# One more key operand in DRAM, early operands for the second layer, and the last stores on another queue

## The chip, the cores and the metric

The kernel runs on one NeuronCore of a Trainium2 chip. The engines are TensorE (PE, matmuls; PEld is its weight loading), VectorE (DVE), ScalarE (ACT), GpSimd (POOL) and SyncE (SP). SP computes nothing and only issues transfers; POOL computes and also issues transfers. On-chip memory is SBUF, matmul results go to the eight banks of PSUM, and everything larger lies in DRAM. The metric is the time of one execution in microseconds (us), the median over several runs.

## What is computed

The input x has 2048 rows of 1024 columns, all arrays are 32-bit floats. Cut to what matters, the reference is:

```
xn = layernorm(x)
q, k, v = split heads of xn @ wqkv            # 32 heads of 32
pq, pk  = phi(q), phi(k)                      # phi(t) = (t+1 if t>0 else exp(t)) + 1e-6
kv  = pk^T v   per head;   z = sum of pk over rows
s   = (pq kv / (pq . z + 1e-6)) @ wo
h   = silu(xn @ w1) * (xn @ w3)               # 3584 columns
g   = silu(h @ w2)
out = x + s * g
```

## The kernel before

**Precision and products.** Every 32-bit operand is split into a high and a low part. `split` (L91) does this with one ACT instruction (L95, the high part) and one DVE instruction (L96, the low part). A product then takes three matmuls (L103 to L105). On top of that every large product is done in the seven block products of the Strassen-Winograd scheme, whose operands are blocks and sums of blocks (A11, S1 ... on one side, B11, T1 ... on the other; for the row products Y00, R2 ... in place of the B and T).

**Stages, in order of time.** The tokens are taken in two halves (h = 0, 1). For each half the keys, the queries and the hidden layer (gate w1, up w3) are computed by `gemm`. In the second half, after keys and queries, come the *row products* xn^T pk (`row_products`, L558): seven products in the order of `ROWS` (L625), each in four steps over the tokens. Then follow the hidden layer of the second half with the attention's small products beside it, the *attention* product s (the segment "s", 8 token groups m = 0 to 7), and the *second layer* h @ w2 in five segments of the hidden columns, B0 to B4, with the last segment also writing the output.

**The key operands.** `key_rows` (L519) turns each block of phi(k) by TensorE and stores operands of the row products in the DRAM tiles `y_d` through POOL (`keep_keys`, L516): Y00 at the first block, R5 and Y10 at another, Y01, R4 and R2 at the last (L549 to L554). Y00 is made at L536 in a buffer of the pool called `small` (tag "c", six buffers of 128x512). Those six also serve the intermediate results c22, c21 and c12 of `gemm`, r2, the results of the attention product, and raw operands of the second layer. The pool hands a buffer to its next user when its last user is done.

**The row products' loads.** A step of a row product loads two tiles of x operands and two of key operands with two transfers on SP's queue (`load`, L564) into one of two "raw" buffers, and splits them into eight smaller buffers (`ready`, L580). The last row product needs A11 and R2 − Y00. Y00 is loaded beside R2 into a "job" buffer (named yy; four such buffers, shared with the small jobs of the stage), and POOL subtracts it (L583) before the split. The loads named qd (L882, L884) and pqd (L847) belong to small jobs of the attention that run beside; wg is the first gate weight of the second half and uses a "raw" buffer too.

**Order.** The source is traced in order, and a planner then plays it through a simulated time line. On each engine it places the earliest traced instruction that is ready at that moment, and hands out buffers in this simulated order. So a load traced later can be issued earlier when its buffer is free. Each engine then executes its list strictly in order; SP's list holds most loads, POOL's most stores.

**From the attention to the second layer.** `Segment.right(k)` (L1016) splits seven right operands for the block k; `Segment.operands(m)` (L1023) loads and splits the seven left operands of the token group m. The first group of a segment runs "outer": for each k all seven products into seven banks. The right operands of the attention lie in the pool `pa`. The first seven of the second layer were traced after the attention (L1272), in the pool `pw`, which is laid over `pa`, `praw` and `st` after these are closed (L1260). `ask_first` (L1161) only requested four of the seven raw operands during the last attention group.

**The end.** `finish` (L1191) runs four times for each token group in the last segment, in the order (t, n) = (1,1), (0,0), (1,0), (0,1). It loads s and x (ss, xs), applies silu on ACT, multiplies and adds on DVE, and stores through POOL (L1202, or L1204, where the transfer itself adds).

Of the kernel before, what the change touches and what calls it, by code (L numbers as in the profile page):

```python
# [9 lines left out]
F32 = mybir.dt.float32  # L10
FR = mybir.dt.float32r
# [5 lines left out]
P = 128  # L17
C = 512
# [4 lines left out]
def tile_linear_attention_times_swiglu(  # L23
# [10 lines left out]
    nc = tc.nc  # L34
# [47 lines left out]
    s_d = [dram.tile([P, D], F32, name=f"s_d{t}") for t in range(S // P)]  # L82
    AOPS = ["A11", "S2", "S3", "S1", "A12", "A22", "S4"]
    XS = ["A11", "A12", "S1", "S3", "A22", "S2", "S4"]
    YS = ["Y00", "Y01", "Y10", "R5", "R2", "R4"]
    x_d = [dram.tile([P, TH // 2, len(XS), C], F32, name=f"x_d{h}") for h in range(NH)]
    y_d = [dram.tile([P, TH // 2, len(YS), ND // 2, P], F32, name=f"y_d{h}") for h in range(NH)]
    g_d = [dram.tile([P, ND // 2, C], F32, name=f"g_d{n}") for n in range(4)]
# [19 lines left out]
    pb = ctx.enter_context(tc.tile_pool(name="pb", bufs=8))  # L108
    pe = ctx.enter_context(tc.tile_pool(name="pe", bufs=3))
    pc = ctx.enter_context(tc.tile_pool(name="pc", bufs=6))  # L110
    era1 = ExitStack()
    pa = era1.enter_context(tc.tile_pool(name="pa", bufs=1))
    praw = era1.enter_context(tc.tile_pool(name="praw", bufs=2))
    st = era1.enter_context(tc.tile_pool(name="st", bufs=2))

    def small(name):
        return pc.tile([P, C], F32, tag="c", name=name)
# [4 lines left out]
    def job_tile(shape, name):  # L122
        return praw.tile(shape, F32, tag="job", bufs=4, name=name)
# [392 lines left out]
    def keep_keys(h, pair, n, t):  # L516
        nc.gpsimd.dma_start(out=y_d[h][:, :, YS.index(n), pair], in_=t.rearrange("p (t d) -> p t d", d=P))  # L517

    def key_rows(h, pair):  # L519

        rows = {}

        def use(n, c, src):
            j = 2 * pair + n
            pk = signed(f"pk{h}_{j}_{c}")
            z = st.tile([P, 1], F32, tag="z", name="z")
            phi(src, pk, z)
            nc.vector.scalar_tensor_tensor(zacc[:, j:j + 1], z, C * 1e-6, zacc[:, j:j + 1],
                                           op0=ALU.add, op1=ALU.add)
            later.append([3, lambda: turn(n, c, pk)])  # L530

        def turn(n, c, pk):
            V = nc.vector
            p_ = turned(pk, f"k{h}_{pair}_{n}{c}")
            if (c, n) == (0, 0):
                y00 = small(f"y00_{h}_{pair}")  # L536
                nc.scalar.activation(y00, p_, AF.Identity, bias=eps)  # L537
                keep_keys(h, pair, "Y00", y00)
            elif (c, n) == (1, 1):
                rows["y01"] = job_tile([P, 2, C], f"y01_{h}_{pair}")  # L540
                nc.scalar.copy(out=rows["y01"][:, 1], in_=p_)
            elif (c, n) == (1, 0):
                y10, r5 = (rows.setdefault("y10", job_tile([P, 2, C], f"y10_{h}_{pair}"))[:, e] for e in range(2))
                nc.scalar.activation(y10, p_, AF.Identity, bias=eps)
                V.tensor_sub(out=r5, in0=rows["y01"][:, 1], in1=p_)
                keep_keys(h, pair, "Y10", y10)
                keep_keys(h, pair, "R5", r5)
            else:
                (y01, r4), r5, r2 = (rows["y01"][:, e] for e in range(2)), rows["y10"][:, 1], small(f"r2_{h}_{pair}")  # L549
                nc.scalar.activation(y01, p_, AF.Identity, bias=eps)  # L550
                V.scalar_tensor_tensor(r4, p_, 2e-6, r4, op0=ALU.add, op1=ALU.add)
                V.scalar_tensor_tensor(r2, p_, 1e-6, r5, op0=ALU.add, op1=ALU.add)
                for n_, t in (("Y01", y01), ("R4", r4), ("R2", r2)):
                    keep_keys(h, pair, n_, t)  # L554

        return use

    def row_products():  # L558
# [3 lines left out]
        steps = [(i, *k) for i in range(len(ROWS)) for k in ks]  # L562

        def load(i, h, t):  # L564
            x_, y_, less = ROWS[i]
            raw = praw.tile([P, 4, C], F32, tag="raw", name=f"xy{i}_{h}{t}")

            def rows(dst, n):
                src = y_d[h][:, t:t + 2, YS.index(n)].rearrange("p t j d -> p t (j d)")
                nc.sync.dma_start(out=dst, in_=src)  # L570

            nc.sync.dma_start(out=raw[:, :2], in_=x_d[h][:, t:t + 2, XS.index(x_)])
            rows(raw[:, 2:], y_)
            other = None
            if less:
                other = job_tile([P, 2, C], f"yy{i}_{h}{t}")
                rows(other, less)
            return raw, other

        def ready(i, h, t):  # L580
            raw, other = data[i, h, t]
            if other is not None:
                nc.gpsimd.tensor_sub(out=raw[:, 2:], in0=raw[:, 2:], in1=other)  # L583
# [14 lines left out]
        for at, s in enumerate(steps):  # L598
# [408 lines left out]
    class Segment:  # L1007
# [5 lines left out]
            self.place, self.right_of, self.left_of, self.acc, self.end = place, right, left, acc, end  # L1013
            self.Y, self.X = {}, {}

        def right(self, k):  # L1016

            for i, n in enumerate(PRODUCTS):
                raw = self.right_of(n, i, k)
                self.Y[n, k] = self.place(n, i, k)  # L1020
                split(self.Y[n, k], raw)
# [141 lines left out]
            ask(i, n, k, small)  # L1163
        return asked[i, n, k]

    def ask_first():
# [21 lines left out]
    def added_by_dma(m, t):  # L1188
        return m < ADDED and t == 1

    def finish(m, t, n, a):  # L1191
        r0, cols = (2 * m + t) * P, slice(n * C, (n + 1) * C)
        ss = small(f"ss{m}_{t}{n}")
        nc.sync.dma_start(out=ss, in_=s_d[2 * m + t][:, cols])
        if not added_by_dma(m, t):
            xs = small(f"xs{m}_{t}{n}")
            nc.sync.dma_start(out=xs, in_=x[r0:r0 + P, cols])
        nc.scalar.activation(a, a, AF.Silu)
        nc.vector.tensor_mul(a, a, ss)
        if not added_by_dma(m, t):  # L1200
            nc.vector.tensor_add(a, a, xs)
            nc.gpsimd.dma_start(out=out[r0:r0 + P, cols], in_=a)  # L1202
        else:
            nc.gpsimd.dma_start(out=out[r0:r0 + P, cols], in_=a, accum_op=ALU.add)  # L1204

# [52 lines left out]
    assert all(next(j, None) is None for j, _ in jobs)  # L1258
# [17 lines left out]
    acc.extend(pw.tile([P, 2, 2, C], F32, tag=f"acc{m}", name=f"acc{m}") for m in range(NG))  # L1276
# [25 lines left out]
```

## Time and profile before

| what | value |
|---|---|
| median of 3 runs | 2360.43 us (2357.89 to 2363.99) |
| the profiled execution | 2364.7 us |
| its span, first to last instruction | 2362.9 us |
| mean granted TensorE clock | 0.992 |
| DRAM traffic | 308.81 MB read, 172.49 MB written |
| row products | about 917 to 1093 us of the span |
| attention product | about 1655 to 1809 us |
| second layer | 1809 to 2352 us |

The profile lists busy times by engine, then groups of instructions by source line, and who waited for whom. In a timeline a row has the start, the duration (of several merged instructions where "x4" stands), engine, line, operation, output and inputs, and in square brackets how long the engine was idle just before and what ended that. SPq is the queue in which SP issues transfers. Rows of stretches ("100.00:200.00") have the busy time of PE, PEld, DVE, ACT and POOL with their numbers of instructions, the granted clock of TensorE, the share of the DMA engines and GB/s.

### The profile page before, as it was taken

What the parts mean: (1) busy time and instruction counts of PE and PEld (TensorE: products, weight loads), DVE (VectorE), ACT (ScalarE), POOL (GpSimd) and SP (SyncE); (2) the same over time, 40 slices, a digit from 0 to 9 for tenths busy, and PEclk for the clock granted to TensorE, in tenths of its full rate; (3) what the DMA queues carried; (4) which work ended last, traced back from release to release, by engine and by line L of the source; (5) the groups of instructions that cost most, each with busy time, mean ns of one, the idle gap of its engine ahead of it and who ended that gap; (6) DMA issues with size and microseconds to landing.
All of it is one profiled execution on the core that took longest, in us unless ns stands there. A gap on an engine that the chain in (4) does not pass through costs nothing.

```text
span 2362.9 us, 30966 instructions
## 1 busy us (share of the span) xinstructions
PE 2306.2 (98%) x10368; PEld 1893.2 (80%) x10368; DVE 1775.7 (75%) x2822; ACT 924.5 (39%) x1639; POOL 697.2 (30%) x852
## 2 busy tenths in 40 slices
PE   6999999999999999998999999999999999999998
PEld 5788878888887888776888888888887788888876
DVE  8887888898877775656867688887745666767798
ACT  5555343423232555433233332334324534342433
POOL 5120433377866111012423435342310000000033
PEclk9999999999999999999999999999999999999999
DMA  6555455576669546776665567665756565766688
GB/s 236 165 174 178 156 179 183 172 228 220 225 210 321 196 134 205 255 257 207 201 193 181 188 200 218 195 216 168 230 153 195 181 198 172 225 208 182 191 265 260
DMA packets 354015, 479.69 MB, mean 203 GB/s; under 512 B 24144, under 2 KB 262736, under 8 KB 353744
## 3 DMA queue, kind: packets, MB, share of 16 engines
q1 hardware_dynamic: 316608, 359.20, 48.1%
q0 software_dynamic: 37248, 118.52, 15.2%
q8 instruction: 81, 1.33, 0.2%
q14 instruction: 78, 0.64, 0.1%
HBM read 308.81 MB, written 172.49 MB: 204 GB/s over the span
## 4 chain that ended last, share of the span: by engine, by line
PE 74%; DMA 5%; DVE 5%; issue 2%; ACT 1%; SPq 1%; POOL 0%; DVEq 0%; POOLq 0%; ACTq 0%
PE g L103 2%; PE g L104 2%; PE g L105 2%; PE cB L103 1%; PE cB L104 1%; PE cB L105 1%; PE dB L103 1%; PE dB L104 1%; PE dB L105 1%; PE aB L105 1%; PE aB L103 1%; PE aB L104 1%; DMA rA12B<-h_d 1%; PE bB L105 1%; PE bB L103 1%
## 5 line engine op out<-in xcount | busy, mean ns | idle before, releaser
L756 POOL DMA_DIRECT2D h_d<-sg x112 | 82.7, 739 | 262.5 <-DVE sg L752 183.9
L1069 POOL DMA_DIRECT2D u_d<-uB x32 | 17.3, 541 | 407.9 <-DVE uB L1052 354.8
L96 DVE TENSOR_TENSOR xy<-xy,xy 128x512 fp32r<-128x512 f32 x112 | 75.0, 704 | 70.4 <-ACT xy L95 70.2
L95 ACT CAST xy<-xy 128x512 fp32r<-128x512 f32 x112 | 65.1, 620 | 109.3 <-PE g L105 62.5
L103 PE MATMUL g<-xy,xy 128*128 128x512 f32 x224 | 82.3, 403 | 7.1 <-ACT xy L95 7.1
L104 PE MATMUL g<-xy,xy 128*128 128x512 f32 x224 | 88.5, 395 | 0.0
L105 PE MATMUL g<-xy,xy 128*128 128x512 f32 x224 | 87.9, 393 | 0.0
L517 POOL DMA_DIRECT2D y_d<-y x40 | 28.6, 718 | 141.9 <-ACT y L537 81.6
L1052 DVE TENSOR_TENSOR acc<-cB,acc 128x512 f32<-128x512 f32 x50 | 34.4, 688 | 40.2 <-PE cB L105 40.2
L1052 DVE TENSOR_TENSOR acc<-dB,acc 128x512 f32<-128x512 f32 x56 | 38.5, 688 | 31.0 <-PE dB L105 30.8
L736 POOL TENSOR_TENSOR hs<-hs,sg 128x256 f32<-128x256 f32 x56 | 61.1, 1090 | 0.1
L103 PEld LDWEIGHTS g<-xy,xy 128*128 128x128 f32 x224 | 42.1, 190 | 21.9 <-ACT xy L95 9.6
L738 POOL TENSOR_TENSOR hs<-sg 128x256 f32<-128x256 f32 x56 | 57.7, 1031 | 0.0
L894 POOL DMA_DIRECT2D qs_d<-qd x32 | 18.0, 564 | 119.3 <-DVE qd L890 82.0
L1183 POOL DMA_DIRECT2D s_d<-s x32 | 17.3, 541 | 117.7 <-DVE s L1052 70.9
L735 POOL TENSOR_TENSOR hs<-sg,sg 128x256 f32<-128x256 f32 x56 | 50.8, 906 | 1.2
L104 PEld LDWEIGHTS g<-xy,xy 128*128 128x128 f32 x224 | 42.7, 190 | 9.9 <-issue 0.8
L739 POOL TENSOR_TENSOR hs<-sg,hs 128x256 f32<-128x256 f32 x56 | 49.9, 892 | 1.5
L105 PEld LDWEIGHTS g<-xy,xy 128*128 128x128 f32 x224 | 42.6, 190 | 9.2
L771 POOL TENSOR_TENSOR w<-w 128x256 f32<-128x256 f32 x28 | 28.2, 1006 | 70.9 <-DMA w<-in_B_w 69.7
L764 POOL DMA_DIRECT2D h_d<-hs x60 | 45.8, 765 | 4.3 <-POOL hs L739 2.4
L674 POOL DMA_DIRECT2D pq_d<-pq x32 | 17.5, 546 | 91.1 <-DVE pq L507 88.3
(5315 smaller groups left out, 8330.1 us busy)
## 6 DMA issues: line engine op xcount, KB each, us to landing
h_d<-hs POOLq DMA_DIRECT2D x60, 256.0 KB, 3.5
h_d<-sg POOLq DMA_DIRECT2D x56, 256.0 KB, 3.9
w<-in_B_w SPq DMA_DIRECT2D x56, 256.0 KB
wt_d<-w SPq DMA_DIRECT2D x28, 512.0 KB
xy<-x_d SPq DMA_DIRECT2D x28, 512.0 KB
xy<-y_d SPq DMA_DIRECT2D x28, 512.0 KB
h_d<-hs SPq DMA_DIRECT2D x52, 256.0 KB
qs_d<-qd POOLq DMA_DIRECT2D x32, 384.0 KB, 3.9
```

The source lines that it names most:

```text
L95: nc.scalar.copy(out=hi, in_=src)
L96: return nc.vector.tensor_sub(out=lo, in0=src, in1=hi.bitcast(F32))
L103: nc.tensor.matmul(acc, lhsT=wh, rhs=ah, start=start, stop=False, skip_group_check=True)
L104: nc.tensor.matmul(acc, lhsT=wh, rhs=al, start=False, stop=False, skip_group_check=True)
L105: return nc.tensor.matmul(acc, lhsT=wl, rhs=ah, start=False, stop=stop, skip_group_check=True)
L735: e.tensor_add(out=s1, in0=a21, in1=a22)
L736: e.tensor_sub(out=s2, in0=s1, in1=a11)
L738: e.tensor_sub(out=s3, in0=a11, in1=a21)
L739: e.tensor_sub(out=s4, in0=a12, in1=s2)
L756: nc.gpsimd.dma_start(out=h_d[i][2 * h + c][:, 2 * n:4 * n + 2, k], in_=src)
L764: queue.dma_start(out=h_d[i][2 * h + c][:, 6 + 4 * e:10 + 4 * e, k], in_=o[e].rearrange("p (e s) -> p e s", s=P))
L1052: return V.tensor_add(out=c, in0=src, in1=c)
```

## The change

Four things are done together. (1) The key operand R6 = R2 − Y00 is computed on DVE in `key_rows`, in place in y00's buffer, and stored as a seventh operand in `y_d`; the row products no longer load Y00 beside R2 and POOL no longer subtracts. (2) `pa` is placed on the other side of SBUF and stays open during the attention, while `praw` and `st` are closed before it. In their place opens `pw0`, which has room for the second layer's seven right operands of k = 0 and the first accumulator. They are loaded and split during the attention groups 2 to 6, one or two in each. (3) In the last attention group four raw operands of k = 1 are requested, where it was k = 0. (4) In `finish`, the stores of (1,0) and (0,1) of the last token group go through SP's queue, and the two factors of the very last one are requested one call earlier.

```diff
-    YS = ["Y00", "Y01", "Y10", "R5", "R2", "R4"]
+    YS = ["Y00", "Y01", "Y10", "R5", "R2", "R4", "R6"]
...
-    era1 = ExitStack()
-    pa = era1.enter_context(tc.tile_pool(name="pa", bufs=1))
+    era1, era2 = ExitStack(), ExitStack()
+    pa = era2.enter_context(tc.tile_pool(name="pa", bufs=1, side="right"))
...
-                y00 = small(f"y00_{h}_{pair}")
+                y00 = rows["y00"] = small(f"y00_{h}_{pair}")
...
+                V.tensor_sub(out=rows["y00"], in0=r2, in1=rows["y00"])
+                keep_keys(h, pair, "R6", rows["y00"])
...
-            other = None
-            if less:
-                other = job_tile([P, 2, C], f"yy{i}_{h}{t}")
-                rows(other, less)
-            return raw, other
+            return raw
...
-            raw, other = data[i, h, t]
-            if other is not None:
-                nc.gpsimd.tensor_sub(out=raw[:, 2:], in0=raw[:, 2:], in1=other)
-            out = []
+            raw, out = data[i, h, t], []
...
-    ROWS = [("A22", "Y10", None), ("A12", "Y00", None), ("S2", "R2", None), ("S1", "R4", None),
-            ("S3", "R5", None), ("S4", "Y01", None), ("A11", "R2", "Y00")]
+    ROWS = [("A22", "Y10"), ("A12", "Y00"), ("S2", "R2"), ("S1", "R4"), ("S3", "R5"), ("S4", "Y01"), ("A11", "R6")]
...
-        def right(self, k):
-
-            for i, n in enumerate(PRODUCTS):
+        def right(self, k, some=range(7)):
+
+            for i in some:
+                n = PRODUCTS[i]
                 raw = self.right_of(n, i, k)
...
-            ask(0, n, 0, place)
+            ask(0, n, 1, place)
...
+    factors = {}
+
+    def fetch(m, t, n):
         r0, cols = (2 * m + t) * P, slice(n * C, (n + 1) * C)
-        ss = small(f"ss{m}_{t}{n}")
+        ss, xs = small(f"ss{m}_{t}{n}"), None
...
+        factors[m, t, n] = ss, xs
+
+    def finish(m, t, n, a):
+        r0, cols = (2 * m + t) * P, slice(n * C, (n + 1) * C)
+        if (m, t, n) not in factors:
+            fetch(m, t, n)
+        if (m, t, n) == (NG - 1, 1, 0):
+            fetch(m, 0, 1)
+        ss, xs = factors[m, t, n]
+        queue = nc.sync if m == NG - 1 and t != n else nc.gpsimd
...
-            nc.gpsimd.dma_start(out=out[r0:r0 + P, cols], in_=a)
+            queue.dma_start(out=out[r0:r0 + P, cols], in_=a)
...
-    run(attention, ahead=ask_first)
...
-    era1.close()
-    pw = ctx.enter_context(tc.tile_pool(name="pw", bufs=1, reuse_waits="tile"))
+    pw0 = ctx.enter_context(tc.tile_pool(name="pw0", bufs=1, reuse_waits="tile"))
+    pw = []
...
-        return pw.tile([P, 2, C], FR, tag=f"{n}_{k}", name=f"{n}_{k}")
+        return (pw[0] if k else pw0).tile([P, 2, C], FR, tag=f"{n}_{k}", name=f"{n}_{k}")
...
-    layers[0].right(0)
+
+    def first_weights(m):
+        if 2 <= m < NG - 1:
+            layers[0].right(0, [i for i in range(7) if i * 5 // 7 == m - 2])
+
+    run(attention, ahead=ask_next, around=first_weights)
     layers[0].operands(0)
+    era2.close()
+    pw.append(ctx.enter_context(tc.tile_pool(name="pw", bufs=1, side="right", reuse_waits="tile")))
...
```

More of the change, by code (lines that the diff above doesn't have):

```diff
@@ L564, in load @@
         def load(i, h, t):
-            x_, y_, less = ROWS[i]
+            x_, y_ = ROWS[i]
             raw = praw.tile([P, 4, C], F32, tag="raw", name=f"xy{i}_{h}{t}")
@@ L1164, in second_weights, with ask_next @@
         return asked[i, n, k]
-    def ask_first():
+    def ask_next():
         for n, place in zip(PRODUCTS, (spare, spare, small, small)):
-            ask(0, n, 0, place)
+            ask(0, n, 1, place)
     def spare(name):
@@ L1189, in added_by_dma @@
         return m < ADDED and t == 1
-    def finish(m, t, n, a):
+    factors = {}
+    def fetch(m, t, n):
         r0, cols = (2 * m + t) * P, slice(n * C, (n + 1) * C)
-        ss = small(f"ss{m}_{t}{n}")
+        ss, xs = small(f"ss{m}_{t}{n}"), None
         nc.sync.dma_start(out=ss, in_=s_d[2 * m + t][:, cols])
@@ L1256, in tile_linear_attention_times_swiglu @@
         attention.right(k)
-    run(attention, ahead=ask_first)
-    assert all(next(j, None) is None for j, _ in jobs)
+    era1.close()
     jobs.clear()
-    era1.close()
-    pw = ctx.enter_context(tc.tile_pool(name="pw", bufs=1, reuse_waits="tile"))
+    pw0 = ctx.enter_context(tc.tile_pool(name="pw0", bufs=1, reuse_waits="tile"))
+    pw = []
     def layer_place(n, i, k):
-        return pw.tile([P, 2, C], FR, tag=f"{n}_{k}", name=f"{n}_{k}")
+        return (pw[0] if k else pw0).tile([P, 2, C], FR, tag=f"{n}_{k}", name=f"{n}_{k}")
     acc = []
@@ L1271, in tile_linear_attention_times_swiglu @@
               for i, (f0, f1) in enumerate(FB)]
-    layers[0].right(0)
+    def first_weights(m):
+        if 2 <= m < NG - 1:
+            layers[0].right(0, [i for i in range(7) if i * 5 // 7 == m - 2])
+    run(attention, ahead=ask_next, around=first_weights)
     layers[0].operands(0)
+    era2.close()
+    pw.append(ctx.enter_context(tc.tile_pool(name="pw", bufs=1, side="right", reuse_waits="tile")))
     for k in range(1, layers[0].nk):
         layers[0].right(k)
-    acc.extend(pw.tile([P, 2, 2, C], F32, tag=f"acc{m}", name=f"acc{m}") for m in range(NG))
+    acc.append(pw0.tile([P, 2, 2, C], F32, tag="acc0", name="acc0"))
+    acc.extend(pw[0].tile([P, 2, 2, C], F32, tag=f"acc{m}", name=f"acc{m}") for m in range(1, NG))
     for i, seg in enumerate(layers):
```

## The prediction

> **What bounds the kernel now.** I read first the page's busy times, then who PE waits for, then the instruction timeline around each wait. The page says that PE is the bound:
>
> ```profile
> PE 2306.2 (98%) x10368; PEld 1893.2 (80%) x10368; DVE 1775.7 (75%) x2822; ACT 924.5 (39%) x1639; POOL 697.2 (30%) x852
> ```
>
> The change removes no matmul, so it can only win PE's idle time (2362.9 − 2306.2 = 56.7 us) and slow matmuls after it. The waits of PE (total, times, longest, in us) show which idle time the change touches:
>
> ```profile
> PE g L103 <- ACT xy L95: 7.1, 2, 6.9
> ...
> PE cB L103 <- ACT XS3B L95: 2.1, 2, 1.7
> ...
> PE T4B L103 <- ACT T L95: 1.2, 1, 1.2
> ...
> PE bg__9128 L103 <- ACT T2g__9056 L95: 1.0, 1, 1.0
> PE B11B L104 <- DVE B L96: 0.9, 1, 0.9
> PE B22B L103 <- ACT B L95: 0.8, 1, 0.8
> ```
>
> The first and fourth rows are the last row product, A11 times (R2 − Y00), and its exit. The other four are the start of the second layer. Of the 2.1 in the cB row only the longest, 1.7, lies there. Around the long wait PE's timeline reads:
>
> ```profile
> 1073.05 1.20 PE L103 MATMUL g<-xy,xy 128*128 128x512 f32 x4 [0.24 <-ACT xy L95]
> ...
> 1085.66 2.07 PE L103 MATMUL g<-xy,xy 128*128 128x512 f32 x4 [6.87 <-ACT xy L95]
> ...
> 1090.72 1.09 PE L103 MATMUL g<-xy,xy 128*128 128x512 f32 x4
> ...
> 1093.48 0.39 PE L103 MATMUL ag__9096<-A,B11g__9047 128*128 128x512 f32 x1
> ```
>
> The first row begins the third of four steps, the second the last. Twelve matmuls start between the second and third row (5.06 us), twelve between the third and fourth (2.76). So after the wait PE also runs slow and loses 5.06 − 2.76 = 2.3 us. This place costs 7.1 + 2.3 + 1.0 = 10.4 us.
>
> The Trainium skill, "TensorE: Matmul & The Clock Gate", section on the clock gate, says that the array drops to half clock after about 3.4 us without work and needs as long to come back. The 0.42 us per matmul after the 6.87 us wait against 0.23 later agrees. By that rule a wait merely shortened below 3.4 us already returns the 2.3 us.
>
> **Why the last step is late.** Timelines of POOL, DVE, SP's queue and ACT:
>
> ```profile
> 1055.64 2.39 POOL L583 TENSOR_TENSOR xy<-xy,yy 128x1024 f32<-128x1024 f32 x1 [16.46 <-DMA xy<-y_d]
> ...
> 1082.63 2.33 POOL L583 TENSOR_TENSOR xy<-xy,yy 128x1024 f32<-128x1024 f32 x1 [8.67 <-DMA xy<-y_d]
> ```
>
> ```profile
> 1058.71 3.35 DVE L96 TENSOR_TENSOR xy<-xy,xy 128x512 fp32r<-128x512 f32 x2 [4.13 <-ACT xy L95]
> ```
>
> ```profile
> 1037.29 0.36 SPq L570 DMA_DIRECT2D yy<-y_d  x1
> ...
> 1055.21 3.20 SPq L570 DMA_DIRECT2D yy<-y_d  x2
> ...
> 1063.29 0.36 SPq L572 DMA_DIRECT2D xy<-x_d  x1
> ...
> 1064.26 0.66 SPq L882 DMA_DIRECT2D qd<-r_d  x1
> ...
> 1071.29 1.08 SPq L572 DMA_DIRECT2D xy<-x_d  x1
> ...
> 1079.98 0.39 SPq L326 DMA_DIRECT2D wg__9019<-in_B_w  x1
> ```
>
> ```profile
> 1081.23 0.62 ACT L95 CAST xy<-xy 128x512 fp32r<-128x512 f32 x1 [7.20 <-DMA xy<-x_d]
> ...
> 1090.22 0.62 ACT L95 CAST B11g__9047<-wg__9019 128x512 fp32r<-128x512 f32 x1 [3.57 <-DMA wg__9019<-in_B_w]
> ```
>
> The last step's load goes out at 1071.29 because its buffer is freed late. Earlier steps wait for the POOL subtraction (2.4 us), and two DVE splits beside it take 3.35 us. It then goes out in the middle of the qd loads and its split starts ten microseconds later (1071.29 to 1081.23); then POOL subtracts again.
>
> **1. R6 stored as an operand.** Removed: four yy loads and four POOL subtractions. In each of the four steps the split starts without them.
>
> - The third step's load (1063.29) should move forward by the subtraction and its DVE delay, about 3 us, to 1060. The last one's buffer is then free when the second step is split, near 1064, and not at 1071. With the same ten microseconds of flight it lands by 1074.5; PE needs it 2.76 × 2 = 5.5 us after it starts the third step at 1073, at 1078.5. So the wait and the slow clock go.
> - yy's buffers come free for the qd loads from 1037 on. These take over yy's traffic there and leave the time of the last two loads.
> - What is late next: the first gate weights wg (1079.98), in the buffer of the third step. They come some nine microseconds earlier, as PE does, so T2g's wait of 1.0 need not vanish. I leave 0.3 of it. Gain: 10.4 − 0.3 = 10.1 us. Ends: 2.3 us (only the last subtraction goes from the last wait, and no load moves) and 10.4.
>
> Added: eight subtractions on DVE, eight stores on POOL, 2 MB written for the 2 MB no longer read. They follow L552; the windows are those around its first and last:
>
> ```profile
> L552 DVE SCALAR_TENSOR_TENSOR r<-trk,y x8: 679/681/682, 103.1 to 908.3; 128x512 f32<-128x512 f32 x8
> ```
>
> ```profile
> 100.00:200.00 100.00, 100.00 (x469) 82.75 (x468) 79.74 (x144) 56.17 (x95) 21.58 (x34) 1.00 0.53 171
> 800.00:900.00 100.00, 100.00 (x462) 82.58 (x461) 76.15 (x137) 55.79 (x95) 17.11 (x26) 1.00 0.41 132
> ```
>
> Eight times 0.68 is 5.4 us of DVE, hidden behind a PE that is 100% busy with DVE at 76 to 80%. Uncovered it would cost those 5.4. The eight stores are 8 × 0.82 = 6.6 us of POOL, at 17 to 22%; queued behind them are only further stores. I charge 0.3 us. y00 also keeps its buffer, one of six, from its own turn to R6's landing. The first and fourth Y00 store and the first R2 store in the first half:
>
> ```profile
> 77.80 0.73 POOL L517 DMA_DIRECT2D y_d<-y  x1 [18.08 <-ACT y L537]
> ...
> 89.83 0.71 POOL L517 DMA_DIRECT2D y_d<-y  x1 [1.86 <-ACT y L537]
> ...
> 104.14 0.82 POOL L517 DMA_DIRECT2D y_d<-r  x1
> ```
>
> A c22 lives from its first to its last use on DVE, about 6.4 us:
>
> ```profile
> 103.83 0.69 DVE L470 TENSOR_TENSOR c22k__1063<-ck__1020,uk__388 128x512 f32<-128x512 f32 x1
> ...
> 109.51 0.68 DVE L507 SCALAR_TENSOR_TENSOR pk<-c22k__1063,pk 128x512 f32<-128x512 f32 x1
> ```
>
> From 90 to 104 four y00 are live at once and two buffers are left for c22, c21, c12 and r2, of which one or two live at a time. It fits with nothing to spare: cost zero, the end a rival below.
>
> **2. First seven operands early.** Before, they wait for the attention's own buffers:
>
> ```profile
> 1806.11 0.62 ACT L95 CAST B<-rB11B 128x512 fp32r<-128x512 f32 x1
> ...
> 1813.17 0.62 ACT L95 CAST T<-rT4B 128x512 fp32r<-128x512 f32 x1 [2.22 <-DMA rT4B<-wt_d]
> ```
>
> ```profile
> 1809.08 0.68 DVE L96 TENSOR_TENSOR B<-rB11B,B 128x512 fp32r<-128x512 f32 x1
> ```
>
> ```profile
> 1829.31 0.38 SPq L1141 DMA_DIRECT2D rS3B<-h_d  x1
> ```
>
> ```profile
> 1700.00:1800.00 100.00, 100.00 (x443) 82.81 (x442) 44.80 (x69) 24.28 (x42) 10.81 (x20) 1.00 0.52 151
> ```
>
> Moved are seven loads (SP), seven ACT and seven DVE splits, 0.62 and 0.68 us each, into an attention where DVE is 45% and ACT 24% busy: 4.8 us of DVE, hidden; uncovered, that much. On SP they stand ahead of the left operands' loads. If one waits there for a small buffer, the next left operand waits too, and PE behind it; I charge 0.3. At the boundary the waits of 0.9, 1.2 and 0.8 = 2.9 us go. Late next is the second set of seven, which now arrives when the first did: first splits at 1809, the sixth (T4) at 1813.2 plus 0.7. PE, from 1809, needs its B11 after 21 matmuls of 0.23 = 4.8 us, at 1813.8, and its T4 15 matmuls later, at 1817. It holds by 3 us. The 1.7 us wait for S3's load is DVE and SP catching up; with 4.8 us less to do I take 1.0 of it. Gain 3.9; ends 0 (the second set takes the waits over) and 4.6.
>
> **3. The end.** The last two adds on DVE, the two stores on POOL, an SP issue and POOL's landing times:
>
> ```profile
> 2355.15 1.29 DVE L1201 TENSOR_TENSOR acc<-acc,xs 128x512 f32<-128x512 f32 x2
> ```
>
> ```profile
> 2356.13 1.14 POOL L1202 DMA_DIRECT2D out<-acc  x2 [2.65 <-DVE acc L1201]
> ```
>
> ```profile
> 2350.87 0.33 SPq L1197 DMA_DIRECT2D xs<-in_A_x  x1
> ```
>
> ```profile
> DMA to landing us min/median/max: 2.3/5.4/7.4
> ```
>
> ```profile
> 1814.26 4.58 DMA rT1B<-wt_d
> ```
>
> POOL ends its second issue at 2357.27; SP can start when the last add ends, 2356.44, and takes 0.33: 2356.77, a gain of 0.5. An SP store's landing is not shown. The nearest SP transfer, a load in traffic, took 4.58. Against POOL's shortest, 2.3, that turns the gain into a loss of 1.8; against its median, 5.4, it adds 0.8. I take 0.5, ends −1.8 and 1.3. The earlier fetch of two factors gains nothing: the multiply waits for ACT there.
>
> The Trainium skill, "DMA: Bandwidth & Descriptors", section "Issuing engines are not separate DMA queues", says that another issuing engine saves only its issue time. That is the 0.5; its table of first-byte latencies (about 1 us from GpSimd, 0.6 from SP) would make it an estimated 0.9. No run here shows an SP store's landing.
>
> **Sum:** 10.1 − 0.3 + 3.9 − 0.3 + 0.5 = 13.9 us. The profiled execution took 2364.7 (span 2362.9 and 1.8 around it), so 2350.8; it lies 4.3 above the median of the runs, 2360.4, whose prediction is 2346.5.
>
> **Rivals.**
> - *The row wait stays in part* (0.15). The qd loads, now earlier, meet the last two steps in SP's queue; for: SP's two yy issues took 3.2 us at 1055, so the queue was full. Against: they replace yy's bytes. With half the 6.9 us wait left and the clock as slow as now, 3.4 + 2.3 = 5.7 of the gain are lost: 2352.2; I put half of this case under 0.3%.
> - *The second set takes over the boundary's waits* (0.10), so that the pre-split does not do what it says: 3.9 less, 2350.4, still faster.
> - *Small buffers run short in the attention* (0.08): a raw operand waits for an s tile's store. At one product (12 matmuls, 2.8 us) in each of five groups it costs 14 us: 2360.5, no change. Against: two of six are free beside four s tiles.
> - *y00 fills the six buffers* (0.09), the slower one. If c22 must wait until R6 has landed, PE waits 0.68 + 0.82 + about 3 us (POOL stores land in 2.3 at least) = 4.5, plus 2.3 of slow clock = 6.8 per pair, eight pairs in the two halves 54 us: 2346.5 + 54 = 2401. It decides from two pairs on (14 us cancel the gain), and from four it is slower by over 0.3%. Against: the count above, and the queries between the keys of the second half.
>
> **Numbers.** The forecast has 0.58, 2341.5 to 2350: its best is 10.4 + 4.6 + 1.3 = 16.3, and runs scatter by 3 us either way (2357.9 to 2364.0). A change under 0.3%, 7.1 us, can hardly be told from none. Faster: 0.58 + 0.10 + half of 0.15 = 0.75; same 0.08 + 0.08 = 0.16; slower 0.09. The range runs from 2341.5 to 2357: it takes in the first two rivals with scatter and leaves out the last two, 0.17.
>
> **What would show it.** No yy load and no POOL subtraction; the last xy load issued before 1068 and no PE wait over 1 us in the last row product; no wait of B11B, T4B or B22B; DVE and ACT fuller between 1720 and 1790 with PE at 100%; SP issuing the last store. I am wrong if PE shows a new wait in the key stages, if the second set is late, or if other boundaries between layers, whose waits hang on the planner's order, move by several microseconds.

## The result, and the profile after

The changed kernel is slower. Its median is 2396.2 us (2394.0 to 2397.0) against 2362.2 us (2357.9 to 2368.6) for the kernel before in the same comparison: a ratio of 1.0135, with a 95% interval of 1.0113 to 1.0157. The profiled execution has a span of 2394.0 us, where it was 2362.9.

The waits that the change aimed at are gone all the same. First the page of the changed kernel (busy us, share of the span, instructions), then three of the rows that are left in its view of waits:

```profile
PE 2358.5 (99%) x10368; PEld 1897.7 (79%) x10368; DVE 1778.6 (74%) x2830; ACT 925.3 (39%) x1639; POOL 692.5 (29%) x854
```

```profile
PE bk__6499 L103 <- ACT T2k__6350 L95: 0.6, 1, 0.6
...
PE g L104 <- DVE xy L96: 0.5, 1, 0.5
...
PE cB L103 <- ACT XS3B L95: 0.2, 1, 0.2
```

The wait of 7.1 us in the last row product is down to 0.5. The rows for T2g, T4B, B11B and B22B are no longer there, and cB has 0.2 in place of 2.1. PE's idle time fell from 56.7 to 2394.0 − 2358.5 = 35.5 us, so 21 us were won. But PE's *busy* time rose from 2306.2 to 2358.5 us, by 52.3, for the same 10368 matmuls: 5.0 ns each on average. 52.3 − 21.2 = 31.1 us is the whole difference of the two spans.

Where do the slow matmuls lie? The view by stretches has the busy time and number of instructions of PE, PEld, DVE, ACT and POOL, then the granted clock, the share of the DMA engines and GB/s. Gate and up products of the first half's hidden layer (400 to 700 us, called the projections from here on) and second layer (1850 to 2250) of the kernel before:

```profile
400.00:700.00 300.00, 299.53 (x1330) 247.65 (x1328) 250.50 (x312) 101.91 (x172) 197.67 (x228) 1.00 0.63 206
1850.00:2250.00 400.00, 400.00 (x1766) 331.35 (x1765) 276.56 (x487) 154.04 (x299) 15.14 (x28) 1.00 0.63 193
```

The same view of the changed kernel, with the attention product between:

```profile
400.00:700.00 300.00, 300.00 (x1290) 241.83 (x1290) 243.91 (x305) 98.55 (x165) 189.85 (x218) 1.00 0.63 204
1700.00:1800.00 100.00, 99.70 (x426) 80.05 (x425) 54.63 (x85) 30.31 (x52) 13.00 (x24) 1.00 0.63 191
1850.00:2250.00 400.00, 399.31 (x1714) 321.85 (x1713) 263.61 (x471) 148.63 (x298) 16.75 (x31) 1.00 0.60 184
```

PE is as busy as before and its clock is full, yet it starts fewer matmuls: 1290 where it was 1330, 426 where it was 443, 1714 where it was 1766. The change adds no instruction between 400 and 700 us, so the cause is not local to the edits. It is also not everywhere. The timeline of the changed kernel, in the attention product and in the row products:

```profile
1749.68 0.39 PE L103 MATMUL as<-wp,XA12s 128*128 128x512 f32 x1
...
1755.76 0.40 PE L105 MATMUL ds<-wp,XS4s 128*128 128x512 f32 x1
```

```profile
1074.70 0.39 PE L104 MATMUL g<-xy,xy 128*128 128x512 f32 x1
...
1079.00 0.39 PE L105 MATMUL g<-xy,xy 128*128 128x512 f32 x1
```

In the attention 26 matmuls start between the two rows' starts, 6.08 / 26 = 0.234 us apart. In the row products it is 19 in 4.30 us, 0.226 apart. The duration shown, 0.39 to 0.40, is the same in both. The row products are the stage in which both operands lie in one pool.

### The profile page after: what moved, and what is told of

Same layout as the page of the kernel before. It is cut to its first block, busy times and chain, and to the rows that moved or that the text cites. A ratio compares the mean times of both kernels' runs of the same rounds, so it can differ in the third digit from the quotient of the medians.

```text
span 2394.0 us, 30980 instructions
## 1 busy us (share of the span) xinstructions
PE 2358.5 (99%) x10368; PEld 1897.7 (79%) x10368; DVE 1778.6 (74%) x2830; ACT 925.3 (39%) x1639; POOL 692.5 (29%) x854
## 4 chain that ended last, share of the span: by engine, by line
PE 91%; DVE 4%; DMA 3%; issue 1%; ACT 1%; SPq 1%; DVEq 0%; ACTq 0%
PE g L103 2%; PE g L104 2%; PE g L105 2%; PE dB L104 2%; PE dB L103 2%; PE cB L103 2%; PE dB L105 2%; PE aB L105 2%; PE cB L105 2%; PE cB L104 2%; PE aB L104 2%; PE aB L103 2%; PE bB L103 1%; PE bB L105 1%; PE bB L104 1%
## 5 line engine op out<-in xcount | busy, mean ns | idle before, releaser
L750 POOL DMA_DIRECT2D h_d<-sg x112 | 82.8, 740 | 270.0 <-DVE sg L746 175.8
L517 POOL DMA_DIRECT2D y_d<-y x48 | 34.6, 721 | 143.8 <-ACT y L537 82.1
L103 PEld LDWEIGHTS g<-xy,xy 128*128 128x128 f32 x224 | 41.8, 188 | 13.9 <-issue 3.7
L95 ACT CAST XS4B<-rS4B 128x384 fp32r<-128x384 f32 (+1 forms) x40 | 19.7, 492 | 61.7 <-PE cB L105 42.5
```

The source lines that it names most:

```text
L95: nc.scalar.copy(out=hi, in_=src)
L103: nc.tensor.matmul(acc, lhsT=wh, rhs=ah, start=start, stop=False, skip_group_check=True)
L750: nc.gpsimd.dma_start(out=h_d[i][2 * h + c][:, 2 * n:4 * n + 2, k], in_=src)
```

## The experiments

The addresses below are those at which the allocator places the pools, in bytes of a partition. A matmul has a *stationary* operand, loaded as weights; here these lie in the pool `pb` (L108), which begins at byte 17,984 in both kernels. The *moving* operand lies in `pa` or `pw`; in the change that of the second layer's block k = 0 lies in `pw0`, on the left. Before, `pa` begins at 77,376 on the left side. With `side="right"` it ends at the right end, byte 229,344, and as it holds 7 × 16,384 bytes it begins at 114,656. In the row products both operands lie in `pb`. No trace shows these addresses. The 59,392 bytes from `pb` to `pa` before can be added up from the pools in the source (8 × 4,096 + 3 × 2,048 + 10 × 2,048), and b_pad416 below counts on from there.

**First set: alignment, side, or order?** Theory A: 114,656 is no multiple of 64, 77,376 is one, and a moving operand off a multiple of 64 is read more slowly. Rival B: the right side itself is the cause. Rival C: the new order of the work is (more VectorE and ScalarE work beside the matmuls). An unused tile at the right end, of 32, 64 or 96 bytes, shifts the pool:

```diff
+    edge = ctx.enter_context(tc.tile_pool(name="edge", bufs=1, side="right"))
+    edge.tile([P, 8], F32, name="edge")        # 8, 16 or 24 floats
     pa = era2.enter_context(tc.tile_pool(name="pa", bufs=1, side="right"))
```

> The changed kernel with an unused 32-byte tile at the right end of SBUF, so that pa and later pw start at byte 114624 (a multiple of 64) and not at 114656 (32 past one). Theory A, matmuls are slower when the moving operand does not start on a multiple of 64 bytes: 8232 of the 9792 matmuls of 512 columns get back some 6.4 ns each, 53 us, so about 2343 us, with a spacing of 0.227 us between matmuls as in the kernel before. Rival B, the right side of SBUF itself is slow, by its place and not its alignment: no change, 2396 us, spacing 0.233. Rival C, the slowness comes from the new order of instructions: no change, 2396 us.

> The changed kernel with an unused tile of 64 bytes in the same place: pa moves by twice as much but stays 32 past a multiple of 64. Theory A: no change, 2394 to 2398 us, spacing 0.233. If a shift as such helped, because neighbouring addresses or the planner's order change: about 2343 us as with 32 bytes.

> The changed kernel with 96 bytes: pa starts on a multiple of 128, where the kernel before and the variant with 32 bytes start 64 past one. Theory A with 64 bytes as the unit: 2343 us as with 32 bytes. If 128 bytes were the unit and 64 past one only half good: faster than with 32 bytes, spacing below 0.226, each 0.005 us worth 41 us.

In the kernel before, 8 floats fewer in an unused tile among the constants shift all pools by 32 bytes, so that both operands leave the multiples of 64:

```diff
-    const.tile([P, 79], F32, name="gap")
+    const.tile([P, 71], F32, name="gap")
```

> The kernel before with its unused tile of 79 numbers made 71, so that every later tile moves down by 32 bytes and all operands, moving and stationary, start 32 past a multiple of 64. Nothing else changes. Theory A: all 9792 matmuls lose about 6.4 ns, 63 us: about 2425 us, with the row products slow too (spacing 0.233, in the changed kernel 0.227). Rivals B and C: no change, 2362 us.

Measured, against 2364.0 us for the kernel before: 2385.9 us with 32 bytes (ratio 1.0090, 1.0075 to 1.0105), 2391.8 with 64 (1.0114, 1.0099 to 1.0129), 2363.3 with 96 (0.9996, 0.9986 to 1.0006), and 2365.0 for the kernel before, shifted (1.0005, 0.9996 to 1.0015). The view by stretches of the kernels with 32 and with 96 bytes:

```profile
400.00:700.00 300.00, 300.00 (x1301) 243.37 (x1300) 247.15 (x309) 100.81 (x169) 192.63 (x223) 1.00 0.63 204
```

```profile
400.00:700.00 300.00, 299.51 (x1317) 245.60 (x1316) 249.41 (x310) 101.62 (x171) 199.96 (x228) 1.00 0.63 204
```

All three explanations fall. An aligned moving operand (32 bytes) is still slow, and a misaligned one (the kernel before, shifted) is not slow at all, so A is out. Side and order are the same in the three shifted kernels (PE and SP execute the same list), yet the time moves by 28 us among them, so neither B nor C can be the cause of that. What did stay the same in the shifted kernel before is the *distance* between the two operands. That gives theory D: the distance between moving and stationary operand sets the spacing of matmuls. Before, it is 77,376 − 17,984 = 59,392 = 232 × 256; in the change 114,656 − 17,984 = 96,672 = 377 × 256 + 160. All tiles in both pools are whole multiples of 512 bytes, so each pair of operands in them has the same remainder. From here on this remainder is called the distance: 0 before, 160 in the change. (The expectations still count it modulo 512.)

**Second set: the distance alone.** The first kernel keeps all of the change and brings the distance back to 0 with 416 bytes at the right end; a small tile moves into the constants to make room. The second has nothing of the change but its distance:

```diff
 # a_edge416, on the changed kernel
-    const.tile([P, 79], F32, name="gap")
+    const.tile([P, 63], F32, name="gap")
+    mom_c = const.tile([P, TH, 2], F32, name="mom")
...
+    edge.tile([P, 104], F32, name="edge")
     pa = era2.enter_context(tc.tile_pool(name="pa", bufs=1, side="right"))
...
-            mom = st.tile([P, TH, 2], F32, tag="mom", bufs=1, name="mom")
+            mom = mom_c
```

```diff
 # b_pad416, on the kernel before
-    const.tile([P, 79], F32, name="gap")
+    const.tile([P, 63], F32, name="gap")
...
+    shift = ctx.enter_context(tc.tile_pool(name="shift", bufs=1))
+    shift.tile([P, 104], F32, name="shift")
     pa = era1.enter_context(tc.tile_pool(name="pa", bufs=1))
```

> The changed kernel with an unused tile of 416 bytes at the right end of SBUF, so that the moving operands lie a whole number of 2048 bytes from the stationary ones, as in the kernel before (to make room, the 64-byte tile mom is taken from the gap of the constants). Theory D (what slows the matmuls is the distance between moving and stationary operand, modulo 512 bytes: 0 before, 416 in the change): matmul starts 0.226-0.227 us apart in every stage, as before; PE busy back at 2306-2310 us; and the waits stay gone, so the time is that of before less the 21 us by which PE's idle time shrank in the change: 2340-2348 us. Rival E (the distance is one cause, but the denser VectorE and ScalarE work beside the attention product is another): the attention stage stays at 0.229 us or more, and the time is 2352-2363 us.

> The kernel before with an unused tile of 416 bytes ahead of the moving operands' pool, on the left side where that pool was (64 bytes of it taken from the gap of the constants): nothing of the change in it but the distance of 416 bytes modulo 512. Theory D: matmul starts 0.232 us apart in the projections and 0.2335-0.2355 in attention and layers, PE busy up by some 45-55 us, time 2405-2418 us, slower than the change itself, since before's waits are still there. Rival E and every rival that blames the side, the order or the neighbours: 2358-2368 us, spacing 0.2267.

The changed kernel at distance 0 took 2343.0 us against 2363.3 for the kernel before: ratio 0.9917, 0.9902 to 0.9932. The kernel before at the change's distance took 2416.2 us: ratio 1.0227, 1.0212 to 1.0242. Busy times and stretches of the first:

```profile
PE 2299.1 (98%) x10368; PEld 1890.0 (81%) x10368; DVE 1779.0 (76%) x2830; ACT 923.3 (39%) x1639; POOL 687.5 (29%) x854
```

```profile
400.00:700.00 300.00, 300.00 (x1332) 248.17 (x1331) 251.72 (x311) 101.76 (x172) 194.50 (x228) 1.00 0.64 208
1850.00:2250.00 400.00, 400.00 (x1766) 331.04 (x1764) 284.00 (x490) 149.71 (x287) 22.91 (x34) 1.00 0.64 197
```

and of the second:

```profile
PE 2364.9 (98%) x10368; PEld 1896.7 (79%) x10368; DVE 1776.4 (74%) x2822; ACT 925.9 (38%) x1639; POOL 694.6 (29%) x852
```

```profile
400.00:700.00 300.00, 300.00 (x1291) 241.35 (x1290) 242.84 (x307) 98.40 (x166) 190.94 (x220) 1.00 0.61 203
1850.00:2250.00 400.00, 397.86 (x1696) 319.15 (x1696) 266.01 (x476) 156.49 (x312) 16.21 (x30) 1.00 0.61 191
```

The matmul counts of the projections follow the distance: 1332 with the whole change at distance 0, 1291 without any of the change at the change's distance (1330 and 1290 above). As the first has the side and the order of the change, B and C are out altogether. Rival E, VectorE's load beside the matmuls, asked for 2352 us or more at distance 0 and falls too. The effects add up: 2416.2 − 2363.3 = 52.9 us from the distance, 2363.3 − 2343.0 = 20.3 us back from the rest, together 32.6 slower, where 34.0 was measured.

Two further distances, with 352 and 224 bytes at the right end:

```diff
+    edge.tile([P, 88], F32, name="edge")       # a_edge352; 56 in a_edge224
```

> The changed kernel with 352 bytes at the right end: distance 64 modulo 512. Theory D does not say by itself how the cost runs with the distance. If any distance but 0 costs like those run so far (384, 352 and 416: spacing 0.230-0.235), 2380-2396 us. If the cost falls as the distance leaves the weights' end (320 gave 2363 us), it is cheap here: 2343-2365 us. Rival E as for a_edge416, 2352 us or more in any case.

> The changed kernel with 224 bytes at the right end: distance 192 modulo 512. As for the distance of 64: 2380-2396 us if every distance but 0 costs the same, 2343-2365 us if distances that are far from 352-416 are cheap, as 320 was.

They took 2364.1 us (1.0002, 0.9992 to 1.0011) and 2390.5 us (1.0112, 1.0095 to 1.0128). So not every distance but 0 costs the same: 64 costs about 21 us against distance 0, 192 about 47.

**Third set: whose distance, and with what period?** In the kernel before, only the pool of the stationary operands is moved, 192 bytes down; every other pool stays:

```diff
-    const.tile([P, 79], F32, name="gap")
+    const.tile([P, 31], F32, name="gap")
...
     pb = ctx.enter_context(tc.tile_pool(name="pb", bufs=8))
+    shift = ctx.enter_context(tc.tile_pool(name="shift", bufs=1))
+    shift.tile([P, 48], F32, name="shift")
```

> The kernel before with its stationary operands' pool moved 192 bytes down (the gap of the constants is cut by 192 bytes and an unused tile of 192 bytes follows the pool): the moving operands and every other pool keep their addresses, and all operands of the matmuls stay on multiples of 64 bytes. Theory D with the stationary operand as the partner: spacing 0.231 us in the projections and 0.233 us in attention and layers, as in the changed kernel at a distance of 192, and 2400-2412 us; the row products, whose two operands move together, stay at 0.226-0.227. If the partner is not the stationary operand but what VectorE, ScalarE or the DMAs touch in the other pools (rival F), the distance to those is as before: 2358-2368 us.

It took 2409.7 us, ratio 1.0197 (1.0182 to 1.0212). Its stretch in the projections:

```profile
400.00:700.00 300.00, 300.00 (x1295) 241.57 (x1294) 245.03 (x307) 98.88 (x166) 192.09 (x220) 1.00 0.63 204
```

1295 matmuls, as in the changed kernel at the same distance (1296). The moving operands had kept their addresses and their distance to the other pools, so rival F falls. One form of it is left, as VectorE and ScalarE also write into `pb`. A stretch of the same run in which neither they nor GpSimd work, and two of its matmuls:

```profile
466.85:470.15 3.30, 3.30 (x16) 2.67 (x15) 0.00 (x0) 0.00 (x0) 0.00 (x0) 1.00 0.37 108
```

```profile
466.72 0.40 PE L103 MATMUL cg__3940<-A,T4g__3840 128*128 128x512 f32 x1
...
470.22 0.39 PE L103 MATMUL dg__3941<-S,B22g__3868 128*128 128x512 f32 x1
```

Fifteen matmuls start in 3.50 us, 0.233 apart, as in the rest of that run. So the partner is the stationary operand. The row products, whose two operands moved together, kept the mean of the kernel before, 0.228. The period is tested with 160 bytes at the right end, where the distance modulo 512 is 256:

```diff
+    edge.tile([P, 40], F32, name="edge")       # a_edge160
```

> The changed kernel with 160 bytes at the right end: distance 256 modulo 512. Distances of 64 and 320 gave the same spacing in each stage (0.227 and 0.229 us), which speaks for a period of 256 bytes: then 256 is as good as 0, spacing 0.2267, and the time 2340-2348 us. If the period is 512 bytes, a distance of 256 puts the two streams half a weight row apart and costs like 192 or 352: 2380-2396 us.

It took 2344.1 us, ratio 0.9915 (0.9902 to 0.9928), and its row has the count of distance 0:

```profile
400.00:700.00 300.00, 299.97 (x1331) 248.05 (x1330) 248.53 (x310) 101.45 (x172) 195.79 (x228) 1.00 0.64 207
```

So among the distances tried the period is 256 bytes. All kernels of the three sets by the distance, with the matmuls between 400 and 700 us, and the mean from one matmul's start to the next in the attention, where every moving operand lies in `pa` (586 to 588 intervals; waits left out):

| distance | matmuls in 300 us | mean in the attention, us | kernels | time of the changed kernel at that distance |
|---|---|---|---|---|
| 0 | 1325 to 1332 | 0.227 | before, before shifted by 32, change with 416, with 160 | 2343.0, 2344.1 us |
| 64 | 1317, 1318 | 0.229 | change with 96, with 352 | 2363.3, 2364.1 |
| 96 | 1296 | 0.233 | change with 64 | 2391.8 |
| 128 | 1301 | 0.233 | change with 32 | 2385.9 |
| 160 | 1290, 1291 | 0.234 | change, before with 416 | 2396.2 |
| 192 | 1296, 1295 | 0.233 | change with 224, before with `pb` moved | 2390.5 |

**The same inside one kernel.** In the changed kernel `pw0` opens on the left, where `praw` began, at 77,376: its distance is 0. The second layer starts with 21 matmuls from `pw0`. Ahead of them stands the attention (`pa`), behind them block k = 1 (`pw`), both at 160:

```profile
1832.61 0.39 PE L103 MATMUL ds<-wp,XS4s 128*128 128x512 f32 x1
...
1835.19 0.40 PE L105 MATMUL ds<-wp,XS4s 128*128 128x512 f32 x1
...
1836.58 0.39 PE L105 MATMUL T2B<-T,XS2B 128*128 128x512 f32 x1
...
1839.97 0.39 PE L105 MATMUL B22B<-B,XS4B 128*128 128x512 f32 x1
1840.20 0.40 PE L103 MATMUL B11B<-B,XA11B 128*128 128x512 f32 x1
...
1841.84 0.40 PE L103 MATMUL T1B<-T,XS1B 128*128 128x512 f32 x1
```

Eleven intervals in the first 2.58 us are 0.235 each, fifteen between 1836.58 and 1839.97 are 0.226, and seven behind them 0.234. The first three from `pw0` are still 0.231 to 0.235, so a change of pool is felt for some matmuls. Later in the layer matmuls from `pw0` mostly come three at a time between those from `pw`, and there the mixture costs too. At distance 64 the layer of a_edge352 starts 1728 matmuls where a_edge416 starts 1766, 0.2315 us apart on average:

```profile
1850.00:2250.00 400.00, 400.00 (x1728) 324.50 (x1727) 272.47 (x479) 149.74 (x290) 14.59 (x27) 1.00 0.61 190
```

About 9 of the 21 us that distance 64 costs lie in this layer (548.0 us from its first to its last matmul, 539.4 in a_edge416).

**What the parts are worth at distance 0.** Two kernels undo one part each on a_edge416. The first splits the second layer's first operands after the attention again, the second forms R2 − Y00 on GpSimd again:

```diff
 # e416_no_early
-            ask(0, n, 1, place)
+            ask(0, n, 0, place)
...
-    run(attention, ahead=ask_next, around=first_weights)
+    run(attention, ahead=ask_next)
+    layers[0].right(0)
```

```diff
 # e416_no_r6
-                V.tensor_sub(out=rows["y00"], in0=r2, in1=rows["y00"])
-                keep_keys(h, pair, "R6", rows["y00"])
...
+            if less:
+                other = job_tile([P, 2, C], f"yy{i}_{h}{t}")
+                rows(other, less)
...
+            if other is not None:
+                nc.gpsimd.tensor_sub(out=raw[:, 2:], in0=raw[:, 2:], in1=other)
...
-    ... ("S4", "Y01"), ("A11", "R6")]
+    ... ("S4", "Y01", None), ("A11", "R2", "Y00")]
```

> The changed kernel at distance 0, with the second layer's first seven operands split after the attention product again (places kept). By the prediction's term the early splits are worth 3.9 us less 0.3: 2345-2349 us, with waits of 0.9 + 1.2 + 0.8 us before the first matmuls of the layer. If most of the 20 us that the change brings at distance 0 come from here, 2353 us or more.

> The changed kernel at distance 0, with the key operand R6 formed from R2 and Y00 on GpSimd again. By the prediction's terms R6 is worth 10.1 us less 0.3: 2350-2355 us, with the wait of some 7 us before the last step of the row products back, and half the clock behind it. If the wait alone counts and not the slow clock, 2349 us.

They took 2347.0 us (0.9927, 0.9916 to 0.9939) and 2356.7 us (0.9970, 0.9958 to 0.9981). Against the 2343.0 of a_edge416, from the second set, the early operands are worth 3.9 us and R6 13.7; by the ratios to the kernel before of each set, 0.0010 and 0.0053, it is 2.4 and 12.5. The intervals of the ratios leave some 4 us either way, so the part of the early operands is not told from nothing by the medians alone. The traces are sharper: from its first B11B matmul to its last matmul the second layer takes 543.5 us without the early operands (1790.82 to 2334.27) and 539.4 with them, 4.1 less. Of the other kernels at distance 0, two without early operands took 543.7 and 543.4 us (before, before shifted), two with them 536.8 and 538.0 (a_edge160, e416_no_r6). Waits came back at and shortly behind the start of the layer (1796 and 1824 us), though not the same ones as before (line numbers are one higher here). Without the early operands:

```profile
PE T4B L104 <- ACT T L96: 2.0, 1, 2.0
...
PE dB L104 <- ACT XS4B L96: 1.1, 1, 1.1
```

and without R6, where the first and third row are those of the prediction:

```profile
PE g L104 <- ACT xy L96: 7.2, 2, 6.6
...
PE cg__2661 L104 <- DVE c22g__2693 L473: 2.1, 1, 2.1
...
PE bg__9132 L104 <- ACT T2g__9060 L96: 1.1, 1, 1.1
```

For R6, 2356.7 us lies above the expected 2350 to 2355: the 12.5 to 13.7 us stand against some 7 to 12. Where the rest comes from is read off below.

## Why the prediction was wrong, and where it was right

The forecast was 2346.5 us and "faster"; measured was 2396.2, outside the range. **The step that failed** is the sentence under the first row: "The change removes no matmul, so it can only win PE's idle time". Apart from slow matmuls behind waits, it took the busy time of PE as fixed. The change moved `pa` to the other side, the distance to `pb` went from 0 to 160 modulo 256, and PE's busy time grew by 52.3 us. The side of `pa` was in the diff, but it had no term in the sum, no rival, and none of the signs of being wrong that the prediction names. The slower rival, that y00 fills the six buffers, named nearly this time (2401) with another mechanism, by chance: the stretches it spoke of are full, and only their matmul counts fell (469 and 462 before):

```profile
100.00:200.00 100.00, 100.00 (x458) 81.13 (x457) 79.95 (x145) 55.49 (x93) 24.38 (x38) 1.00 0.55 178
800.00:900.00 100.00, 100.00 (x452) 80.98 (x451) 78.56 (x139) 55.40 (x94) 21.11 (x32) 1.00 0.44 139
```

**The other steps** can be judged at distance 0, where only they are left. There the change gave 20.3 us by the medians and 22.2 by the spans, where 13.9 was predicted. The starts of five matmuls, first in the kernel before, then in a_edge416, show in which stage:

```profile
917.64 0.39 PE L103 MATMUL g<-xy,xy 128*128 128x512 f32 x1
...
1673.44 0.39 PE L103 MATMUL as<-wp,XA11s 128*128 128x512 f32 x1
...
1808.27 0.39 PE L103 MATMUL B11B<-B,XA11B 128*128 128x512 f32 x1
...
2351.99 0.39 PE L105 MATMUL dB<-B,XS4B 128*128 128x512 f32 x1
```

```profile
912.18 0.39 PE L104 MATMUL g<-xy,xy 128*128 128x512 f32 x1
...
1078.99 0.39 PE L104 MATMUL ag__9104<-A,B11g__9055 128*128 128x512 f32 x1
...
1657.25 0.39 PE L104 MATMUL as<-wp,XA11s 128*128 128x512 f32 x1
...
1791.21 0.39 PE L104 MATMUL B11B<-B,XA11B 128*128 128x512 f32 x1
...
2330.57 0.39 PE L106 MATMUL dB<-B,XS4B 128*128 128x512 f32 x1
```

(The row for ag in the kernel before, 1093.48, stands in the prediction.)

| stretch | before | a_edge416 | won | predicted |
|---|---|---|---|---|
| start to the row products | 917.6 | 912.2 | 5.5 | −0.3 |
| row products | 175.8 | 166.8 | 9.0 | 9.4, with the slow clock |
| hidden layer, second half | 580.0 | 578.3 | 1.7 | 0.7, of T2g's wait |
| attention | 134.8 | 134.0 | 0.9 | −0.3 to 0 |
| second layer | 543.7 | 539.4 | 4.4 | 3.9 |
| last matmul to the end | 10.9 | 10.1 | 0.8 | 0.5 |

- *R6.* Its place in the row products was right, wait and slow clock, within 0.4 us. So was the way to it. The stage's last x load goes out at 1061.24, where it was 1071.29. Of these 10.05 us the earlier start of the stage makes 5.5, so 4.6 are won (the prediction had 7), and the load's split starts at 1070.89, 9.65 us behind it (predicted ten).

  Too small was the term as a whole: 10.1 − 0.3 against 12.5 to 13.7. The missing part lies ahead of the row products, where the first row-product matmul starts at 912.2 with R6 and at 919.8 without it. Single traces scatter here: of the kernels at distance 0, three with R6 start it between 911.6 and 912.2, three without between 915.4 and 919.8. The row of e416_no_r6:

```profile
919.82 0.39 PE L104 MATMUL g<-xy,xy 128*128 128x512 f32 x1
```

  Two waits of the kernel before lie there, at 302 us (c22g) and at 759 (T2k), each followed by matmuls at half clock. With R6 they are shorter (1.65 in place of 2.12 us, 1.75 in place of 2.25), and the clock stays full behind both. The stretches right behind them, before and in a_edge416:

```profile
302.00:305.00 3.00, 2.94 (x7) 2.36 (x8) 3.00 (x6) 0.63 (x1) 0.00 (x0) 0.50 0.56 172
762.00:766.00 4.00, 4.00 (x11) 3.13 (x10) 4.00 (x5) 3.10 (x7) 3.49 (x4) 0.50 1.06 402
```

```profile
301.80:304.80 3.00, 3.00 (x14) 2.46 (x15) 2.85 (x5) 0.63 (x1) 0.00 (x0) 1.00 0.55 174
759.00:763.00 4.00, 4.00 (x19) 3.32 (x18) 4.00 (x5) 3.25 (x7) 3.69 (x5) 1.00 1.06 396
```

  Why R6 shortens waits in stages that only gained a subtraction and a store is not shown by these runs. VectorE's order differs from 104 us on, PE's only from 811, so a shifted order of the planner is likely, but it was not tried.
- *The clock rule* that stood beside the sum, from the Trainium skill, "TensorE: Matmul & The Clock Gate", Part 1 (the clock drops after about 3.4 us without work), is not borne out as a threshold. Here 2.12 us without work were followed by a granted clock of 0.50, and 1.65 were not. Nor does the length of one wait decide it: in a_edge416 a wait of 1.52 us at 2252, with two of 0.3 in the next 2.4 us, was followed by 0.50, and in the kernel before one of 1.56 at 2274, with two of 0.4 and 0.5, was followed by full clock. The two stretches:

```profile
2255.40:2256.40 1.00, 1.00 (x4) 0.81 (x3) 1.00 (x3) 0.06 (x1) 0.00 (x0) 0.50 0.98 361
```

```profile
2277.00:2281.00 4.00, 4.00 (x19) 3.29 (x18) 4.00 (x9) 1.27 (x2) 0.34 (x1) 1.00 1.02 274
```

  The prediction's inference that a wait shortened below 3.4 us already gives the slow clock back does not hold.
- *Early operands.* Predicted 3.9 less 0.3, measured 2.4 to 3.9 by the medians and 4.1 between the two traces. The second set did not take the waits over, and the attention did not run out of small buffers.
- *The end.* Predicted 0.5; the last add of the change ends at 2388.42 (2387.13 + 1.29) and the span 5.6 us later, where it was 2356.44 and 6.5. That is 0.9 us, all of it in the traces; the medians can't tell it. The last add and the two stores in the changed kernel:

```profile
2387.13 1.29 DVE L1208 TENSOR_TENSOR acc<-acc,xs 128x512 f32<-128x512 f32 x2
2387.84 0.94 SPq L1209 DMA_DIRECT2D out<-acc  x2
```

  In eight further kernels with these stores the span ends 5.6 us after the last add too; only e416_no_r6 ends 3.1 after it, so a landing can also be much shorter. SP ends its second issue 0.36 us after the add, POOL did 0.83 after. So some 0.5 of the gain is the issue and 0.4 the landing; by the rule of the Trainium skill, "DMA: Bandwidth & Descriptors", section "Issuing engines are not separate DMA queues", that only issue time is saved, it would have been 0.5 alone, and by the estimate from that page's latencies 0.9.

## What to carry to other kernels

Moving a pool is not free of cost: compare the addresses of moving and stationary operands before and after, and where matmuls look like those of this kernel, keep the distance on a multiple of 256 bytes, if need be by an unused tile. A PE that is 100% busy at full clock can still be slow. Its share of busy time does not show it; the number of matmuls in a full stretch, or the spacing of their starts, does. When a time moves against a sum of waits, split the difference of the spans into idle and busy time first; here that pointed at the cause at once.

## What the runs showed of the hardware

Matmuls of 512 columns in 32-bit operands, each with its own weights, start 0.227 us apart when the moving operand lies a multiple of 256 bytes from the stationary one, 0.229 at a remainder of 64, and 0.232 to 0.234 at 96 to 192 (means of the attention and the projections), with the clock at 1.00. (300 us by the matmul counts gives some 0.001 to 0.002 less, as 16 of these matmuls have only 128 columns.) The absolute address, the side and the alignment to 64 bytes do not matter by themselves. The cost is not symmetric: a remainder of 64 is cheap and one of 192 is not. Where matmuls at 0 and at 64 take turns, as in the second layer of a_edge352, the mean is 0.232, more than at either alone.

The Trainium skill, "TensorE: Matmul & The Clock Gate", section "Step-by-step: what each phase is for", says that PE reads moving and stationary operand through two independent ports, and that loading the next weights takes no bandwidth from the running matmul. The runs differ: b_pb192 moved the weights alone, and the matmuls came 0.006 us further apart (300 / 1330 to 300 / 1295). That the two reads collide in the memory is the nearest explanation, but it is argued only: no run separated a matmul from the loading of the next weights. Untried are also the remainders 32 and 224 and other operand widths.
